# A constant-matmul warm-up and a new order table for windowed attention with a gated convolution

## The chip, the cores and the metric

The kernel runs on one core of a Trainium2 chip. Its metric is device time in microseconds: the median of several executions. One more execution is profiled. The profile's times count from its first instruction, and its span, 239.8 us here, is a little shorter than the time of that execution, 241.62 us.

## The reference

Four batches, eight heads, 768 positions, head width 64. Every query sees its neighbours at a distance under 16 and, for each of 24 blocks of 32 keys, one summary: the maximum of the block's keys, and the mean of its values. The heads side by side are the input `x` (512 wide) of the second half: a causal convolution of five taps in each channel gives a gate, and the gated value product goes through an output product.

```python
k_sum = k.reshape(B, H, nb, 32, D).max(axis=3)
v_sum = v.reshape(B, H, nb, 32, D).mean(axis=3)
s_l = where(abs(i - j) < 16, scale * q @ k.T, -1e9)
s_s = scale * q @ k_sum.T + log(32)
a = softmax(concatenate([s_l, s_s], -1))
attn = a @ concatenate([v, v_sum], 2)
x = attn.transpose(0, 2, 1, 3).reshape(B, S, H * D)
gate = sigmoid(sum(conv_w[t] * xp[:, t:t + S] for t in range(5)))
out = (gate * (x @ w_val)) @ w_out
```

## The kernel before

The work is cut into 12 groups `g` (four batches, three stretches of 256 positions), and each group into two units `u` of four heads. Every unit and group passes through the same steps, and each step has a letter. The letters with their numbers stand in one long table, `ORDER`, and the program is emitted in that order: each engine executes its own instructions in the order of the table, so the table is the schedule. There is no other planner at run time; semaphores make an instruction wait for its inputs and for its buffer.

The steps of a unit are: `S` scores on TensorE (two halves), `N` mask and row minimum on VectorE (four steps, each of two masked scores), `E` exponentials with row sums on ScalarE (four steps of two), `R` sum and reciprocal on VectorE, `M` normalisation on POOL, `T` transposes on TensorE, `C` their copies on ScalarE, `X` the product with the values on TensorE, then on ScalarE `F` and `H` (two copies of the result) and `I` (the last convolution tap), and `A` on VectorE (the four further taps of each of two halves, eight steps). `G` is the gate on ScalarE. The steps of a group are: `V` the value product (two halves), `gf` gate times value on VectorE, `gh` and `gl` its split into two parts on ScalarE and POOL, `O` the output product (two halves), `oe` its eviction and `st` its store. Group 0 uses plain float32 products. For it the convolution of the first unit is a matmul, `Z`.

Beside these run the preparations: `k`, `q0`, `q`, `v`, `n`, `w`, `o`, `c`, `m`, `i` are loads on SyncE's queue; `ks` is the block maximum of a piece of keys on VectorE and `kc` copies it beside the keys on POOL; `VB` sums the first batch's values with a matmul against a constant of ones, `vb` copies the sums; `tr` sums the values of later batches on POOL or VectorE; `wvs`, `wvd`, `wve` (and `wos`, `wod`, `woe`) turn one quarter of the float64 value (output) weights into float32: a ScalarE step, then a VectorE step that takes the low bits (line 356), then a VectorE step that joins both (line 366). `O.0.1` and `O.0.0` need all four joins of the output weights.

A piece of keys is 478 KB, a quarter of the first queries 128 KB, the mask 180 KB, the convolution weights 20 KB. The first product of scores, `S.0.0`, needs `k.0.0`, its maximum copied beside it, and `q0.0`.

## Time and profile before

| | us |
|---|---|
| median of three runs | 242.12 |
| lowest and highest | 240.76, 245.85 |
| the profiled execution | 241.62 |
| its span | 239.8 |
| TensorE busy | 224.0 |
| ScalarE busy | 186.4 |
| VectorE busy | 171.5 |
| POOL busy | 152.6 |

Busy time is the time in which an engine has an instruction in work; for TensorE, whose matmuls are pipelined, a group's time is best read from its start to the start of the next. A float32 matmul appears as two records. Below, "PE" is TensorE, "PEld" its weight loads, "DVE" VectorE, "ACT" ScalarE, "SP" SyncE.

### The profile page before, as it was taken

Reading aid. Unit: us, or ns where it says so; the run is one execution under the profiler, and the core shown is the slowest. Engines: PE = TensorE matmul, PEld = TensorE weight load, DVE = VectorE, ACT = ScalarE, POOL = GpSimd, SP = SyncE. Lnnn points to the kernel's source line nnn. Section 1 sums busy time; section 2 is a strip of 40 time slices with the busy share of each in tenths; the row PEclk is TensorE's granted clock in tenths of the full one; section 3 lists DMA queues with packets and bytes.
Section 4 is the critical chain, followed back from the end, with each engine's and each line's share of the span. In section 5 each row is a group of like instructions: output and inputs, shape, how many; then the busy total and the mean of one; then the engine's idle time right before and its main releaser. Section 6 shows DMA issues by size and latency. Waiting matters only on the chain.

```text
span 239.8 us, 7765 instructions
## 1 busy us (share of the span) xinstructions
PE 224.0 (93%) x2880; PEld 187.0 (78%) x2880; DVE 171.5 (71%) x676; ACT 186.4 (78%) x612; POOL 152.6 (64%) x216
## 2 busy tenths in 40 slices
PE   0596999899999999999999999999999999999993
PEld 0233988778489889889879898879889889978982
DVE  1568699899999998788877878848396655264300
ACT  0199989999999999899989999889898863443321
POOL 1219699887998996896986974936238728017400
PEclk9999999999999999999999999999999999999999
DMA  6999998989699847364834836235044131102022
GB/s 176 376 396 405 404 383 257 407 278 389 192 324 326 303 154 208 73 243 115 297 125 122 304 101 197 105 77 178 8 120 174 24 100 44 44 3 105 26 92 87
DMA packets 17318, 46.42 MB, mean 194 GB/s; under 512 B 2400, under 2 KB 3424, under 8 KB 17280
## 3 DMA queue, kind: packets, MB, share of 16 engines
q1 hardware_dynamic: 17280, 45.93, 55.8%
q8 instruction: 23, 0.38, 0.6%
q14 instruction: 15, 0.12, 0.2%
HBM read 37.46 MB, written 6.29 MB: 182 GB/s over the span
## 4 chain that ended last, share of the span: by engine, by line
PE 73%; DMA 11%; DVE 7%; SPq 3%; ACT 2%; issue 1%; POOL 1%; DVEq 0%; ACTq 0%
PE out L580 30%; PE val L551 25%; PE x L471 8%; PE s L401 6%; PE pt L454 4%; DMA k<-in_kT_dram 4%; DMA qbd<-in_qT_dram 3%; DMA vn<-in_vn_dram 3%; DMA v<-in_vw_dram 2%; DVE g L505 2%; DVE sn L417 2%; SPq L325 1%; ACT p L432 1%; DVE wf L366 1%; DVE low_wo L356 1%
## 5 line engine op out<-in xcount | busy, mean ns | idle before, releaser
L505 DVE SCALAR_TENSOR_TENSOR g<-xf,cwt,g 128x256 f32<-128x256 f32 x184 | 89.4, 486 | 27.7 <-ACT g L500 23.3
L432 ACT ACTIVATE p<-sn,nm 128x120 f32<-128x120 f32 x192 | 74.0, 394 | 0.8 <-DVE nm L417 0.8
L445 POOL TENSOR_TENSOR p<-p,nm 128x480 f32<-128x480 f32 x48 | 46.9, 988 | 19.6 <-DVE nm L440 13.4
L551 PE MATMUL val<-xh,wv 128*128 128x256 f32 x352 | 50.0, 284 | 0.0
L417 DVE CUSTOM_DVE_ANT_0 sn<-s,mask 128x120 f32<-128x120 f32 x192 | 43.0, 276 | 5.9 <-PE s L401 4.8
L551 PEld LDWEIGHTS val<-xh,wv 128*128 128x128 f32 x352 | 45.1, 188 | 1.6 <-issue 0.4
L580 PE MATMUL out<-wo,gh 128*128 128x512 f32 x176 | 45.9, 402 | 0.0
L565 POOL TENSOR_TENSOR gl<-gf,gh 128x512 fp32r<-128x512 f32 x22 | 28.4, 1291 | 18.9 <-ACT gh L560 18.9
L491 POOL TENSOR_TENSOR xl<-xf,xh 128x512 fp32r<-128x512 f32 x22 | 28.4, 1290 | 17.9 <-ACT xh L483 15.9
L432 ACT ACTIVATION_READ_ACCUMULATOR p<-sn,nm 128x1 f32 x192 | 38.1, 198 | 0.0
L580 PEld LDWEIGHTS out<-wo,gh 128*128 128x128 f32 x176 | 31.7, 188 | 7.4 <-issue 0.3
L401 PE MATMUL s<-k,qbd 64*64 64x120 f32 x768 | 27.2, 278 | 8.4 <-POOL k L271 8.4
L401 PEld LDWEIGHTS s<-k,qbd 64*64 64x64 f32 x768 | 20.7, 138 | 16.4 <-POOL k L271 8.4
L471 PE MATMUL x<-pts,v 120*64 120x64 f32 x768 | 29.4, 225 | 2.9 <-ACT pts L458 2.9
L471 PEld LDWEIGHTS x<-pts,v 120*64 120x64 f32 x768 | 26.1, 137 | 6.8 <-ACT p L432 2.0
L458 ACT COPY pts<-pt 120x512 f32<-120x512 f32 x48 | 27.7, 588 | 3.7 <-PE x L471 2.3
L282 POOL TENSOR_TENSOR vT<-vT 128x384 f32<-128x384 f32 (+3 forms) x44 | 24.9, 566 | 6.5 <-DMA vT<-in_vT_dram 3.8
L551 PE MATMUL val<-xl,wv 128*128 128x256 f32 x176 | 27.9, 281 | 0.0
L556 DVE SCALAR_TENSOR_TENSOR gf<-gt,val 128x512 f32<-128x512 f32 x24 | 16.3, 683 | 10.8 <-PE val L551 7.4
L551 PEld LDWEIGHTS val<-xl,wv 128*128 128x128 f32 x176 | 23.9, 188 | 0.0
L580 PE MATMUL out<-wo,gl 128*128 128x512 f32 x88 | 23.9, 393 | 0.0
L590 ACT ACTIVATE ob<-out 128x512 f32<-128x512 f32 x23 | 13.9, 604 | 10.9 <-PE out L580 10.6
(58 smaller groups left out, 267.2 us busy)
## 6 DMA issues: line engine op xcount, KB each, us to landing
v<-in_vw_dram SPq DMA_DIRECT2D x24, 512.0 KB
k<-in_kT_dram SPq DMA_DIRECT2D x16, 478.0 KB
out_dram<-ob SPq DMA_DIRECT2D x23, 256.0 KB
qbd<-in_qT_dram SPq DMA_DIRECT2D x11, 512.0 KB
vT<-in_vT_dram SPq DMA_DIRECT2D x12, 384.0 KB
raw_wv<-in_wv_dram SPq DMA_DIRECT2D x4, 512.0 KB
raw_wo<-in_wo_dram SPq DMA_DIRECT2D x4, 512.0 KB
v<-vs SPq DMA_DIRECT2D x36, 48.0 KB
```

The costliest lines, as they stand in the source:

```text
L282: nc.gpsimd.tensor_tensor(dst, src[:, :, :n], src[:, :, n : 2 * n], ALU.add)
L401: nc.tensor.matmul(sp[64 * e : 64 * e + 64, h, c * KW : c * KW + KW], qbd[g % NQB][64 * h : 64 * h + 64, pr, i * QT : i * QT + QT], ktile( ...
L417: nc.vector.tensor_tensor_reduce(sn[:, n, :], tiles["s", u][:, h, c * KW : c * KW + KW], mask[:, mv, :], -1.0 / math.sqrt(D), 3.0e38, ALU.add,
L432: nc.scalar.activation(p[:, n, :], tiles["sn", u][:, n, :], AF.Exp, bias=tiles["nm", u][:, n : n + 1], scale=-1.0, accum_out=rs[:, n, :1],)
L445: nc.gpsimd.tensor_tensor(p[:, w], p[:, w], ri[:, w].unsqueeze(2).broadcast_to([P, TPU, KW]), ALU.mult)
L458: nc.scalar.copy(pts[:, :, QT * e : QT * e + QT], tiles["pt", u][:KW, e])
L471: nc.tensor.matmul(dst, v[:KW, i, c0 : c0 + D], src, start=True, stop=g > 0)
L491: nc.gpsimd.tensor_tensor(xl[:, prs(u), :], xf(g)[:, prs(u), HALO:], tiles["xh", g][:, prs(u), :].bitcast(F32), ALU.subtract,)
L505: nc.vector.scalar_tensor_tensor(gt, xf(u // NHP)[:, pr, o : o + SG], cwt[:, pr, o : o + 1], gt, ALU.mult, ALU.add)
L551: nc.tensor.matmul(ps[:, r], w, x, start=(n == 0), stop=(n == len(terms) - 1))
L565: nc.gpsimd.tensor_tensor(gl[:, cos, :], tiles["gf", g, cp], tiles["gh", g][:, cos, :].bitcast(F32), ALU.subtract)
L580: nc.tensor.matmul(ps, x, w, start=(n == 0), stop=(n == len(terms) - 1))
```

## The change

A new step `D` is added: two float32 matmuls of 104 by 104 on the tile of ones, into the buffer that the transposes use later; nobody reads the result. It is called twelve times, ahead of all other matmuls. The order table is another one altogether; the list of steps in it is otherwise the same, except that one sum of values (`tr.1.3`) goes to VectorE instead of POOL, `tr.2.3` goes to VectorE, and the ScalarE or POOL side of some weight splits is swapped.

```diff
 ORDER = """
-k.0.1 mset c k.0.0 q0.0 k.0.2 q0.1 m n.0.2 cd ks.0.1 q0.2 k.0.3 ks.0.0 n.0.3 q0.3 kc.0.0 kc.0.1
-S.0.0 ks.0.2 n.0.4 w.3 S.0.1 n.0.1 kc.0.2 q.1 VB.2 N.0.2 n.0.5 E.0.2 N.0.1 N.0.0 E.0.0 i N.0.3
...
+k.0.0 mset q0.0 m k.0.1 D.8 i D.11 k.0.2 q0.1 D.10 q0.2 ks.0.0 c D.2 kc.0.0 D.5 n.0.2 D.3 k.0.3
+D.4 D.0 D.9 D.6 D.1 D.7 ks.0.1 q0.3 S.0.0 w.0 N.0.1 kc.0.1 E.0.1 ks.0.2 n.0.0 S.0.1 q.1 n.0.5
...
+    def op_D(i):
+        t = once("warm", lambda: ps_t.tile([P, 2, NP, QT], F32, tag="pt", name="warm"))
+        n = QT + BASE
+        for k in range(2):
+            nc.tensor.matmul(
+                t[:n, k].rearrange("p a b -> p (a b)")[:, :n],
+                tiles["ones"][:, :n], tiles["ones"][:, :n], start=True, stop=True,
+            )
+
...
-        c=op_c, ks=op_ks, kc=op_kc, tr=op_tr, VB=op_VB, vb=op_vb, VS=op_VS,
+        c=op_c, ks=op_ks, kc=op_kc, tr=op_tr, VB=op_VB, D=op_D, vb=op_vb, VS=op_VS,
```

TensorE at the start of the program, first before and then after (`s` are scores, `vb` the sums of the first batch's values, `warm` the new step; in a name the first number is the unit, in `k` the batch and the piece):

```order
L401 MATMUL s_0_122<-k_0_0_99,qbd0_81 64x120 x8
L401 MATMUL s_0_122<-k_0_1_88,qbd0_81 64x120 x8
L296 MATMUL vb_0_150<-vn_1_106,ones_90 64x512
L296 MATMUL vb_1_152<-vn_1_106,ones_90 64x512
L401 MATMUL s_1_173<-k_0_2_102,qbd0_81 64x120 x8
```

```order
L309 MATMUL warm_101<-ones_90 104x104 x24
L410 MATMUL s_0_144<-k_0_0_88,qbd0_81 64x120 x8
L410 MATMUL s_0_144<-k_0_1_99,qbd0_81 64x120 x8
L296 MATMUL vb_0_184<-vn_1_123,ones_90 64x512
L296 MATMUL vb_1_186<-vn_1_123,ones_90 64x512
L410 MATMUL s_1_198<-k_0_2_107,qbd0_81 64x120 x8
L410 MATMUL s_1_198<-k_0_3_127,qbd0_81 64x120 x8
```

The 24 constants stand ahead of the first scores, and both halves of unit 1's scores now follow the first sums together.

TensorE around the first output product `O.0.1` (`out_0_1`), before and after (`val` is `V`, `pt` is `T`, `x` is `X`; lines are nine higher in the new file):

```order
L551 MATMUL val_1_1_951<-xh_1_715,wv_344 128x256 x8
L551 MATMUL val_1_1_951<-xl_1_790,wv_344 128x256 x4
L551 MATMUL val_1_1_951<-xh_1_715,wv_344 128x256 x8
L551 MATMUL val_1_1_951<-xl_1_790,wv_344 128x256 x4
L401 MATMUL s_9_1000<-k_1_2_283,qbd0_81 64x120 x8
L401 MATMUL s_9_1000<-k_1_3_447,qbd0_81 64x120 x8
L454 MATMUL pt_6_1022<-ident_84,p_6_777 120x64 x16
L471 MATMUL x_5_1043<-pts_5_908,v_2_618 64x64 x16
L580 MATMUL out_0_1_1074<-wf_87,gf_0_0_665 128x512 x2
L580 MATMUL out_0_1_1074<-wf_87,gf_0_1_857 128x512 x2
```

```order
L463 MATMUL pt_5_881<-ident_84,p_5_602 120x64 x16
L410 MATMUL s_8_910<-k_1_0_313,qbd0_81 64x120 x8
L410 MATMUL s_8_910<-k_1_1_422,qbd0_81 64x120 x8
L480 MATMUL x_4_937<-pts_4_867,v_2_672 64x64 x16
L589 MATMUL out_0_1_987<-wf_87,gf_0_0_722 128x512 x2
L589 MATMUL out_0_1_987<-wf_87,gf_0_1_821 128x512 x2
L589 MATMUL out_0_0_1003<-wf_87,gf_0_0_722 128x512 x2
L589 MATMUL out_0_0_1003<-wf_87,gf_0_1_821 128x512 x2
L463 MATMUL pt_6_1035<-ident_84,p_6_774 120x64 x16
L480 MATMUL x_5_1058<-pts_5_1013,v_2_672 64x64 x16
L410 MATMUL s_9_1083<-k_1_2_465,qbd0_81 64x120 x8
L410 MATMUL s_9_1083<-k_1_3_530,qbd0_81 64x120 x8
```

Unit 9's scores, unit 6's transposes, unit 5's product and a half of group 1's value product stood ahead of the output product and now stand behind it.

VectorE at the last joins of the output weights (`wf`), before and after (`low_wo` holds the low bits, `g` is a tap):

```order
L356 TENSOR_SCALAR low_wo_2_996<-raw_wo2_846 128x512
L505 SCALAR_TENSOR_TENSOR g_3_976<-xf_1_620,cwt_85,g_3_976 128x256
L366 SCALAR_TENSOR_TENSOR wf_87<-sc_wo2_998,low_wo_2_996 128x512
L356 TENSOR_SCALAR low_wo_1_1041<-raw_wo1_842 128x512
L505 SCALAR_TENSOR_TENSOR g_3_976<-xf_1_620,cwt_85,g_3_976 128x256
L366 SCALAR_TENSOR_TENSOR wf_87<-sc_wo1_992,low_wo_1_1041 128x512
```

```order
L514 SCALAR_TENSOR_TENSOR g_2_748<-xf_1_646,cwt_85,g_2_748 128x256
L365 TENSOR_SCALAR low_wo_3_980<-raw_wo3_871 128x512
L375 SCALAR_TENSOR_TENSOR wf_87<-sc_wo3_967,low_wo_3_980 128x512
L426 ISA sn_8_969,nm_8_970<-s_8_910,mask_83 128x120
```

The last join stood among the taps of unit 3 and now follows the last tap of unit 2.

## Rows read from the trace of the kernel before

**Rows 1.** The page: busy time of each engine with its share of the span, and the granted TensorE clock in 40 slices (9 is 90% of full or more).

```profile
PE 224.0 (93%) x2880; PEld 187.0 (78%) x2880; DVE 171.5 (71%) x676; ACT 186.4 (78%) x612; POOL 152.6 (64%) x216
...
PEclk9999999999999999999999999999999999999999
```

**Rows 2.** The chain of work that ended last, in order of time: start in us, duration in us, engine, tile and line.

```profile
58.77 0.60 DVE wf L366
...
59.51 3.67 PE out L580 x8
63.18 0.98 PE s L401 x32
...
67.79 2.84 PE val L551 x24
70.63 0.61 PE pt L454 x16
...
72.22 1.08 PE x L471 x32
...
225.03 11.16 PE out L580 x48
...
236.26 0.60 ACT ob L590
```

**Rows 3.** TensorE's timeline at the start: start in us, busy us, and in brackets the idle time before and what ended it.

```profile
8.42 2.09 PE L401 MATMUL s<-k,qbd 64*64 64x120 f32 x32 [8.42 <-POOL k L271]
...
13.50 1.74 PE L296 MATMUL vb<-vn,ones 128*64 128x512 f32 x4
15.17 0.64 PE L401 MATMUL s<-k,qbd 64*64 64x120 f32 x16
...
18.59 1.94 PE L296 MATMUL vb<-vn,ones 128*64 128x512 f32 x8
...
23.96 0.34 PE L471 MATMUL x<-pts,v 120*64 120x64 f32 x4 [1.84 <-ACT pts L458]
```

**Rows 4.** Busy time of each engine in three stretches (stretch, its length, PE, PEld, DVE, ACT, POOL, then granted clock, DMA share, GB/s), and VectorE's waits in the first 60 us (us in total, times, longest).

```profile
0.00:59.37 59.37, 47.44 (x792) 35.40 (x792) 45.98 (x209) 46.66 (x171) 38.16 (x71) 1.00 0.95 346
59.51:236.19 176.68, 176.58 (x2088) 151.61 (x2088) 125.34 (x468) 139.02 (x441) 114.29 (x146) 1.00 0.45 145
...
8.42:59.51 51.09, 47.45 (x793) 35.44 (x793) 44.13 (x206) 46.80 (x171) 36.91 (x59) 1.00 0.98 367
...
DVE ks L258 <- DMA k<-in_kT_dram: 4.7, 4, 2.0
DVE cwt L356 <- DMA cwraw<-in_cw_dram: 4.6, 1, 4.6
DVE sn L417 <- PE s L401: 3.1, 5, 1.3
```

**Rows 5.** The timeline of VectorE (first row) and ScalarE (the others): the first masked score, the table load behind it, the first two exponentials, and the first and the last of ScalarE's four small waits up to 35 us.

```profile
10.57 0.28 DVE L417 CUSTOM_DVE_ANT_0 sn<-s,mask 128x120 f32<-128x120 f32 x1 [0.52 <-PE s L401]
...
10.95 1.28 ACT L432 ACT_TABLE_LOAD   x1 [10.95 <-DVE nm L417]
12.24 0.39 ACT L432 ACTIVATE p<-sn,nm 128x120 f32<-128x120 f32 x1
...
12.63 0.38 ACT L432 ACTIVATE p<-sn,nm 128x120 f32<-128x120 f32 x1
...
16.61 0.39 ACT L432 ACTIVATE p<-sn,nm 128x120 f32<-128x120 f32 x1 [0.27 <-DVE nm L417]
...
34.85 0.59 ACT L486 COPY xf<-x 128x512 f32<-128x512 f32 x1 [0.72 <-PE x L473]
```

**Rows 6.** What VectorE's steps take in the chain (a tap before a tap, a masked score, a tap before a masked score, a reciprocal, a block maximum), and from the groups by line the sum of values (count, busy us, mean ns).

```profile
45.44 0.49 DVE g L505
45.93 0.18 DVE sn L417
...
46.32 0.41 DVE g L505
...
52.59 0.20 DVE nm L440
...
53.56 0.86 DVE ks L258
...
L278 DVE TENSOR_REDUCE vsT<-vT 128x24 f32<-128x768 f32 x1 | 0.9, 902 | 0.0
```

**Rows 7.** The start on POOL (the constants) and VectorE (the second and the third block maximum).

```profile
0.98 0.48 POOL L209 MEMSET ones<- 32x1 f32 x4
...
6.91 0.95 DVE L258 TENSOR_REDUCE ks<-k 128x24 f32<-128x768 f32 x1 [1.31 <-DMA k<-in_kT_dram]
...
9.10 0.95 DVE L258 TENSOR_REDUCE ks<-k 128x24 f32<-128x768 f32 x1 [1.24 <-DMA k<-in_kT_dram]
```

**Rows 8.** TensorE's timeline at the float32 product of line 530 and the group behind it, and the weight loads of that product (count, busy us, mean ns).

```profile
27.59 4.58 PE L530 MATMUL g<-xf,dg 128*128 128x256 f32 x20
32.10 0.64 PE L401 MATMUL s<-k,qbd 64*64 64x120 f32 x16
...
L530 PEld LDWEIGHTS g<-xf,dg 128*128 128x128 f32 x20 | 3.7, 189 | 0.6 <-issue 0.2
```

**Rows 9.** The timeline at the end: VectorE's half of the one tile that is evicted in halves.

```profile
233.89 0.42 DVE L588 TENSOR_SCALAR ob<-out 128x256 f32<-128x256 f32 x1 [8.03 <-ACT ob L587]
```

More of the change, by code (lines that the diff above doesn't have):

```diff
@@ new lines @@
+M.0.1 S.2.1 n.1.0 E.1.2 VB.5 N.2.1 n.1.3 M.0.0 E.2.1 N.2.2 VB.1 N.2.3 E.2.3 N.2.0 w.1 wve.0 S.3.0
+E.2.0 k.1.0 R.1 S.3.1 E.2.2 w.3 T.0 M.1.1 N.3.0 VB.4 C.0.0 R.2 N.3.1 v.1.0 C.0.1 M.2.0 VB.3 N.3.3
+wvs.2 N.3.2 wvd.2 M.2.1 v.1.1 S.4.0 vb.1 S.4.1 wve.2 vb.0 M.1.0 T.2 E.3.3 N.4.1 k.1.1 X.0 N.4.0
+wvc.2.1 E.3.2 N.4.2 k.1.2 C.2.0 cs C.2.1 ce N.4.3 W.0 T.1 F.0 tr.1.0.1 E.4.1 S.5.0 S.5.1 tr.1.3
+W.1 n.1.1 wvs.1 Z.0.0 k.1.3 E.3.0 wvd.1 wvc.0.1 E.3.1 wve.1 C.1.0 R.3 Z.0.1 wvs.3 wvd.3 M.3.1
+C.1.1 wve.3 E.4.0 wvb.2 N.5.0 N.5.3 wvc.1 ks.1.0 f.1.1.1 X.1 E.5.0 wvc.3.1 n.1.2 N.5.2 E.5.3
@@ new lines @@
+wos.0 k.2.0 wod.0 k.2.3 S.8.0 H.3 v.3.1 wod.1 S.8.1 E.6.3 L.3 v.3.0 X.4 woe.0 n.2.2 E.7.3 woe.1
+H.4 A.2.6 q.5 woc.1.1 wos.3 N.8.1 A.2.7 tr.2.0 wod.3 G.2 F.4 woe.3 O.0.1 I.3.0 N.8.2 E.7.0 A.3.0
+R.6 E.7.2 O.0.0 A.3.1 M.6.1 ks.2.1 I.3.1 C.5.0 h.2 A.3.2 M.6.0 E.7.1 N.8.0 A.3.3 C.5.1 kc.2.1
+N.8.3 oe.0.1 L.2 A.3.4 woc.3 R.7 T.6 A.3.5 E.8.3 f.3.0.0 M.7.0 X.5 A.3.6 E.8.1 A.3.7 v.4.0 ks.2.3
+S.9.0 G.3 f.3.1.1 S.9.1 I.4.1 ks.2.0 kc.2.3 V.1.0 f.3.1.0 I.4.0 M.7.1 E.8.0 A.4.0 f.3.0.1 A.4.1
+L.4 woc.0 N.9.3 q.6 oe.0.0 A.4.2 k.2.2 C.6.0 st.0.1 A.4.3 E.8.2 V.1.1 N.9.0 A.4.4 H.5 N.9.2 F.5
@@ new lines @@
+st.1.0 O.2.1 F.9 A.8.7 n.3.1 ks.3.0 G.8 L.9 I.9.1 gf.3.0 I.9.0 h.5 N.14.1 E.13.0 M.11.1 A.9.0
+N.14.0 VS.2 E.13.2 L.8 A.9.1 T.11 ks.3.1 oe.2.1 X.10 E.14.2 M.12.1 A.9.2 C.11.0 A.9.3 S.15.0
+M.12.0 E.13.3 A.9.4 S.15.1 V.4.1 gh.3.0 N.15.1 C.11.1 A.9.5 gl.3.0 vs.2 N.15.2 A.9.6 gh.3.1
+f.6.0.0 R.13 kc.3.0 F.10 A.9.7 gl.3.1 q.9 G.9 V.4.0 f.6.0.1 I.10.0 gf.4.1 M.13.1 f.6.1.1 E.14.0
+N.15.0 A.10.0 st.2.1 h.6 M.13.0 N.15.3 I.10.1 f.6.1.0 E.14.1 A.10.1 tr.3.1 T.12 A.10.2 H.10 S.16.0
+A.10.3 E.15.3 S.16.1 A.10.4 E.14.3 X.11 A.10.5 A.10.6 E.15.0 v.7.1 tr.3.2 N.16.1 O.3.0 n.3.3 F.11
@@ new lines @@
+A.15.1 E.18.3 N.19.1 A.15.2 E.19.0 h.8 A.15.3 M.17.1 E.19.3 oe.4.0 S.20.0 gf.6.1 S.20.1 A.15.4
+gh.6.1 T.17 N.20.3 E.19.1 VS.3 A.15.5 V.7.1 N.20.1 vs.3 N.20.2 C.17.0 A.15.6 f.9.1.0 N.20.0 A.15.7
+f.9.0.1 R.18 G.15 st.3.1 E.19.2 S.21.0 f.9.1.1 S.21.1 gh.6.0 f.9.0.0 X.16 C.17.1 gl.6.0 N.21.3
+E.21.3 st.4.0 N.21.0 N.21.1 O.5.1 I.16.0 M.18.0 N.21.2 F.16 E.21.2 A.16.0 gl.6.1 gf.7.1 I.16.1
+H.16 A.16.1 M.18.1 E.21.0 A.16.2 S.22.0 S.22.1 A.16.3 E.21.1 T.18 A.16.4 E.20.3 A.16.5 X.17 N.22.2
+N.22.0 v.10.0 V.7.0 A.16.6 H.17 v.10.1 N.22.1 F.17 A.16.7 C.18.0 R.19 G.16 R.21 M.19.1 oe.5.1
@@ new lines @@
+I.17.0 O.5.0 E.20.0 M.19.0 A.17.0 N.22.3 I.17.1 L.17 C.18.1 A.17.1 E.20.2 A.17.2 L.16 A.17.3
+f.10.1.1 A.17.4 T.19 f.10.0.0 A.17.5 E.22.1 M.21.0 S.23.0 gf.7.0 S.23.1 E.20.1 A.17.6 X.18 E.22.0
+N.23.2 A.17.7 V.8.1 oe.5.0 N.23.0 gh.7.0 N.23.1 st.5.0 R.20 gh.7.1 st.5.1 gl.7.0 f.10.0.1 E.22.2
+f.10.1.0 G.17 M.20.0 O.6.1 H.18 gf.8.1 E.22.3 h.9 gl.7.1 C.19.0 R.22 I.18.1 M.20.1 I.18.0 F.18
+O.7.1 M.21.1 oe.6.1 A.18.0 C.19.1 A.18.1 A.18.2 A.18.3 A.18.4 T.20 A.18.5 E.23.1 X.19 A.18.6
+A.18.7 oe.7.1 N.23.3 V.8.0 C.20.0 st.7.1 G.18 v.11.0 C.20.1 v.11.1 I.19.0 H.19 E.23.0 O.7.0 F.19
@@ L128 @@
+H.22 O.8.0 gf.10.0 A.22.2 A.22.3 V.10.1 gh.10.0 gh.9.1 gl.10.0 I.22.1 oe.8.0 A.22.4 gl.9.1 st.8.0
+A.22.5 X.23 gf.10.1 L.22 A.22.6 O.9.0 F.23 A.22.7 gh.10.1 H.23 gl.10.1 G.22 L.23 O.10.1 oe.9.0
+I.23.0 st.9.0 I.23.1 st.8.1 A.23.0 A.23.1 A.23.2 V.11.0 A.23.3 A.23.4 oe.10.1 A.23.5 A.23.6
+st.10.1 A.23.7 O.9.1 G.23 gf.11.0 V.11.1 oe.9.1 gh.11.0 st.9.1 O.10.0 gf.11.1 gh.11.1 gl.11.1
+gl.11.0 O.11.0 oe.10.0 st.10.0 O.11.1 oe.11.0 st.11.0 oe.11.1 st.11.1
 """
```

111 lines of the change are left out of this document (38 added, 73 removed).

## The prediction

> **What bounds the kernel now.** I read the chain of waits first, in order of time. From 59.51 us to 236.19 us it is TensorE and nothing else: one group of matmuls behind the other, ending with the output product of the last stretch [rows 2]. TensorE is also the busiest engine of the page, at 224.0 us [rows 1]. So the end of the kernel is one sum: the moment at which the first output product (`O.0.1`, line 580) starts, plus the TensorE work that stands behind it in the program, 176.7 us in the kernel before, plus the last eviction and store. What set that moment is the row ahead of it in the chain: VectorE's last join of the output weights (line 366), which started at 58.77 us [rows 2]. Nothing of TensorE itself was late.
>
> The second view is TensorE's own timeline at the start [rows 3]. Its first 32 score records take 2.09 us, and the same 32 take 0.98 us later in the chain [rows 2]; four sum records (line 296) take 1.74 us at 13.50 us, where later eight take 1.94 us. The granted-clock line reads full throughout [rows 1], but by these durations the array ran at 1.2 GHz from 8.42 us to about 14.9 us (by its length some 1.4 us of that group is still slow) and at 2.4 GHz from there on. The work of 8.42 to 15.17 us, 48 score and eight sum records, takes 1.5 + 1.9 us at the later pace, so the slow stretch costs 3.3 us of TensorE time. TensorE was never idle in it.
>
> Then I asked what VectorE and ScalarE were short of before 59.4 us. VectorE worked 45.98 us of the first 59.37 us [rows 4], so it lost 13.4 us: 4.6 us for the first load, 4.7 us for four loads of `k`, 3.1 us for score tiles. ScalarE's first exponential starts at 12.24 us, behind a table load of 1.28 us, and it hardly waits after that: four small waits, 0.2 to 0.7 us each, 1.4 us in all by 35 us [rows 5].
>
> **The change, part by part.** (1) It adds 24 matmuls of 104 columns to TensorE, before the first scores, on constants that POOL has written by 1.46 us [rows 7]. No row shows this shape. The nearest is the full-width float32 product of line 530: ten matmuls (20 records) of 256 columns from 27.59 us to the next group at 32.10 us [rows 8], 0.45 us each, so 0.183 us for 104 columns at 2.4 GHz and 0.37 us at 1.2 GHz. From above: if the weight load (189 ns a record there, two records to a matmul) were not hidden, some 0.35 us more each. I take the lower price, since in line 530 the load is hidden. If the clock needs as long as before, 6.5 us from the first matmul, it rises at 8.1 us: 17.7 matmuls by then, the other 6.3 in 1.15 us. The constants end at 9.2 us; between 7.9 us (the clock rises at 5 us) and 10.4 us (it never does).
>
> (2) It moves the loads: `k.0.0` is first, with queries and mask ahead of the second `k`. In the kernel before VectorE could take the second `k` at 6.91 us, with 976 KB in the queue up to it, and the third at 9.10 us, with 1582 KB [rows 7]. The second is now at 1264 KB, so 7.95 us, and its reduction ends at 8.9 us. The first score tile follows the constants: 9.2 to 9.7 us. The first masked score starts at 9.76 us, the table load 0.38 us behind it (10.57 to 10.95 us before [rows 5]), and the first exponential at **11.4 us instead of 12.24**. It cannot be ahead of 10.6 us (the reduction at 8.9 us) and is at 12.6 us if the clock stays low.
>
> (3) VectorE's start follows ScalarE's. Ahead of the first tap `A.1.0` VectorE has 24.5 us of work in the new order (24 masked pairs 9.6 us, seven reductions of `k` 6.1 us, eight weight steps 5.2 us, two sums of `v` 1.8 us, small ones 1.8 us), and what `A.1.0` waits for, `I.1.0` on ScalarE, has 24.4 us ahead of it (40 exponentials at 0.38 us and 9.2 us of copies). So VectorE loses at least what ScalarE loses: 11.4 us and some 0.2 us of small waits, **11.6 us instead of 13.4**. Ends: 10.6 and 12.8 us.
>
> (4) The order around `O.0.1` is the core. VectorE has less ahead of the last join: four taps (0.45 us each, between the 0.41 us in front of a masked score and 0.49 us in front of a tap), three masked pairs of 0.40 us, one reduction of `k` at 0.87 us, one 0.26 us sum and reciprocal; and one sum of `v` more, 0.90 us [rows 6]. That is 3.2 us less (3.1 to 3.4 us with the cheapest and the dearest taps), so 42.8 us. TensorE loses more cover: scores 9 (0.98 us), transposes 6 (0.61 us), product 5 (1.08 us) and half a value product (2.84 us) [rows 2] now stand behind `O.0.1`, **5.5 us**. So the join comes earlier, and more is left to do behind it.
>
> (5) The tail: the last output tile is now the one that is evicted in two halves beside each other, the longer one 0.42 us [rows 9], instead of 0.60 us [rows 2]. That gives 0.2 us. All other moves I cost at nothing: behind `O.0.1` TensorE is the bound, with 139.0 us of ScalarE and 125.3 us of VectorE work under 176.7 us [rows 4], and by the same counts of work the new order has every producer there at least 2.5 us ahead. SyncE's queue has the last quarter of the output weights as its 48th transfer, as before; its last quarter landed in time for VectorE then, and I cost it at nothing; were it late, VectorE and `O.0.1` would wait as long as it is.
>
> **The sum.** `O.0.1` starts at 42.8 + 11.6 + 0.14 = 54.5 us (59.51 before; 0.14 us from the join's end to the first matmul). Behind it 176.7 + 5.5 = 182.2 us: 236.7 us. The tail is 3.6 - 0.2 = 3.4 us: span 240.1 us, and with the 1.8 us that the profiled execution has around its span (241.62 against 239.8) **241.9 us**. The profiled execution lies 0.5 us under the median of the three runs, 242.12, so the forecast is 0.3 us over the one and 0.2 us under the other: no change. With the ends above it goes from 240.7 to 243.2 us.
>
> **A rule of the Trainium skill.** The row gives 3.3 us for the slow stretch, 1.4% of the span [rows 3]. The Trainium skill (TensorE: Matmul & The Clock Gate, Part 1) says that the array starts throttled until activity releases it, and that for modelling this costs under 1% of a typical kernel. By the row a full return would be 3.3 us, by the page under 2.4 us; the sum above uses neither, because in it the time goes to waiting for VectorE.
>
> **Rivals.** First, *TensorE decides, and the slow stretch comes back.* For it: in the 51.1 us from 8.42 us TensorE idled only 3.6 us [rows 4], so the front is nearly its own. Then 241.6 - 3.3 - 0.2 = 238.1 us, and up to 3.6 us less if the new order also closes its idle time: 234.5 us. Against it: the chain names VectorE ahead of 59.51 us, and 5.5 us of TensorE work was put behind that point.
>
> Second, slower: *TensorE cools in the gap that the new order opens.* The last work ahead of `O.0.1` is `S.8` and `X.4`; `S.8` waits for the masked scores of unit 7, with 37.8 us of VectorE work up to them, so it starts at 37.8 + 11.6 = 49.4 us, and 0.98 + 1.08 us later TensorE has nothing left: from 51.5 us it waits 3.0 us for the join; its longest gap after the start was 1.84 us, at 23.96 us, and the clock held [rows 3]. If the clock falls there, `O.0.1` and `O.0.0` (7.3 us) and the next products run at 1.2 GHz; at the start the same cost 3.3 us: 245.2 us. It decides only if the gap is longer than any in this trace. The Trainium skill (the same page, Why this matters for your kernels) warns of idle gaps between bursts of matmuls; no row here shows a fall.
>
> Third, *the constants do not raise the clock.* They end at 10.4 us, ScalarE starts at 12.6 us, and the sum is 243.1 us; the slow scores are then hidden in the 8 us that TensorE idles before `O.0.1` anyway.
>
> **How the numbers follow.** Forecast 0.55, first rival 0.29, second 0.11, third 0.05. A measurement of this kernel tells about 2% from no change: 237.3 and 247.0 us. Half of the first rival lies under 237.3 us, which gives 0.15 for faster; half of the second, with a second gap like it, over 247.0 us, 0.06 for slower; 0.79 for the same. The range takes in the near end of the first rival and most of the second, and the unknown waits of VectorE (one like its longest for `k`, 2.0 us, would give 243.9 us [rows 4]): 238.0 to 245.0 us.
>
> **What would show it.** Score records of line 410 at about 0.5 us for 16 from the first one on; the constants ending near 9.2 us; the first exponential near 11.4 us; `O.0.1` near 54.5 us with an idle gap of some 3 us in front of it and an unbroken TensorE behind. The prediction is wrong if that gap is missing (VectorE's work is cheaper than priced, or the other rows in front of the join moved), or if TensorE waits a second time after it.

## The result, and the profile after

The changed kernel takes **243.84 us** (median of 18 executions, 241.78 to 246.3); the kernel before, measured beside it, 241.67 us (18 executions). The ratio is **1.0073**, 95% interval 1.0047 to 1.0099: no change at 2%, but slower, where the forecast said no change with a time 0.2 us under the 242.12 us of the three runs. The time lies in the forecast's range. (Ratios here leave out executions over 1.5% above the fastest of their kernel, so they can differ from the quotient of the medians.)

The profiled execution took 242.41 us (span 240.6), 1.4 us *less* than the median; that of before, 241.62 us, was at its median. The page and the chain of the changed kernel, the latter in order of time (start, us, what), answer to [rows 1] and [rows 2]:

```profile
PE 228.6 (95%) x2928; PEld 193.5 (80%) x2928; DVE 172.2 (72%) x678; ACT 186.6 (78%) x612; POOL 147.5 (61%) x206
...
q8 instruction: 23, 0.38, 0.6%
```

```profile
1.50 7.47 PE warm L309 x48
8.98 0.61 PE s L410 x16
...
9.99 1.28 ACT L441
11.29 5.40 ACT p L441 x28
...
53.43 0.68 DVE wf L375
54.16 7.14 PE out L589 x16
...
99.25 5.69 DMA out_dram<-ob
...
228.77 8.30 PE out L589 x36
237.14 0.39 ACT ob L596
```

The start is as reckoned: constants to 8.97 us, scores at the fast pace from the first on (0.61 us for 16 in the chain; 0.64 us in the timeline, as at 15.17 us in [rows 3]), first exponential at 11.29 us, first output product at 54.16 us. But the chain behind it is no longer TensorE alone: at 99.25 us it runs over a store. And the idle gap of 3 us ahead of 54.16 us is missing. TensorE's timeline (start, busy, in brackets the idle time before and what ended it) shows where TensorE idled instead, to be held against [rows 3]:

```profile
12.43 0.64 PE L410 MATMUL s<-k,qbd 64*64 64x120 f32 x16 [0.56 <-issue]
14.13 0.64 PE L410 MATMUL s<-k,qbd 64*64 64x120 f32 x16 [1.06 <-POOL xf L395]
...
23.29 1.21 PE L410 MATMUL s<-k,qbd 64*64 64x120 f32 x32 [0.97 <-DVE low_wv L365]
...
27.11 0.68 PE L463 MATMUL pt<-ident,p 64*120 64x64 f32 x16
29.81 1.05 PE L410 MATMUL s<-k,qbd 64*64 64x120 f32 x32 [2.02 <-DVE low_wv L365]
30.79 4.59 PE L539 MATMUL g<-xf,dg 128*128 128x256 f32 x20
...
105.67 1.22 PE L560 MATMUL val<-xh,wv 128*128 128x256 f32 x8 [0.37 <-ACT ob L599]
...
109.12 1.22 PE L560 MATMUL val<-xh,wv 128*128 128x256 f32 x8 [0.35 <-ACT vs L325]
...
113.99 1.15 PE L480 MATMUL x<-pts,v 120*64 120x64 f32 x32 [0.17 <-ACT xh L492]
```

Two places ask for a reason. The first is **28 us**: 2.02 us of idle time ahead of `S.5`. The view names VectorE's `low_wv`, but `S.5` does not read it. It needs the score buffer, that is, the last masked score of unit 4, and VectorE's timeline has that done at 26.5 us, before `low_wv` starts. The first weight load of `S.5` (the line PEld), the first of its instructions, also ran ahead of the stop:

```profile
26.19 0.28 DVE L426 CUSTOM_DVE_ANT_0 sn<-s,mask 128x120 f32<-128x120 f32 x1
26.39 1.81 DVE L278 TENSOR_REDUCE vsT<-vT 128x24 f32<-128x768 f32 x2
28.11 0.68 DVE L365 TENSOR_SCALAR low_wv<-raw_wv 128x512 uint32<-128x512 uint32 x1
...
27.72 0.13 PEld L410 LDWEIGHTS s<-k,qbd 64*64 64x64 f32 x1
```

The second is **102 to 114 us**. ScalarE's eviction of `O.2.1` waited 2.30 us for a buffer whose store had not landed, and TensorE lost 0.9 us in three pieces behind it:

```profile
105.02 0.60 ACT L599 ACTIVATE ob<-out 128x512 f32<-128x512 f32 x1 [2.30 <-DMA out_dram<-ob]
```

The busy times by stretch (length; PE, PEld, DVE, ACT, POOL; granted clock) answer to [rows 4]: 182.9 us from the first output product to the last matmul, 182.0 of them busy.

```profile
54.16:237.07 182.91, 182.01 (x2192) 156.74 (x2192) 131.54 (x495) 145.74 (x460) 116.26 (x146) 1.00 0.48 152
8.91:54.16 45.25, 39.15 (x690) 29.43 (x689) 38.34 (x181) 40.45 (x152) 29.80 (x48) 1.00 0.98 360
```

That accounts for the profiled execution, 0.8 us over before: 54.16 + 182.0 + 0.9 + 3.5. It does not account for the medians, 2.2 us apart. Each execution comes with its mean granted clock, and there is a hint in them: of the changed kernel's 18 executions nine have a clock of 0.997 or more (median 243.17 us) and nine less, down to 0.976 (median 244.94). Of 29 executions of the kernel before, in the first group of experiments, 24 have 0.997 or more (241.28 us) and five 0.992 or 0.993 (242.88 us). The clock alone is not the difference, since the executions at 0.997 or more are still 1.9 us apart.

### The profile page after: what moved, and what is told of

Same layout as the page of the kernel before. It is cut to its first block, busy times and chain, and to the rows that moved or that the text cites. A ratio compares the mean times of both kernels' runs of the same rounds, so it can differ in the third digit from the quotient of the medians.

```text
span 240.6 us, 7861 instructions
## 1 busy us (share of the span) xinstructions
PE 228.6 (95%) x2928; PEld 193.5 (80%) x2928; DVE 172.2 (72%) x678; ACT 186.6 (78%) x612; POOL 147.5 (61%) x206
## 4 chain that ended last, share of the span: by engine, by line
PE 72%; ACT 12%; DVE 8%; issue 3%; DMA 2%; POOL 2%; ACTq 0%; POOLq 0%; DVEq 0%
PE out L589 26%; PE val L560 25%; PE x L480 8%; ACT p L441 7%; PE s L410 5%; PE pt L463 4%; PE warm L309 3%; DMA out_dram<-ob 2%; DVE sn L426 2%; DVE g L514 2%; ACT pts L467 1%; DVE wf L375 1%; DVE ks L258 1%; POOL vT L282 1%; ACT xh L492 1%
## 5 line engine op out<-in xcount | busy, mean ns | idle before, releaser
L514 DVE SCALAR_TENSOR_TENSOR g<-xf,cwt,g 128x256 f32<-128x256 f32 x184 | 89.3, 485 | 26.5 <-ACT g L509 15.5
L574 POOL TENSOR_TENSOR gl<-gf,gh 128x512 fp32r<-128x512 f32 x22 | 28.3, 1292 | 36.1 <-ACT gh L569 27.8
L426 DVE CUSTOM_DVE_ANT_0 sn<-s,mask 128x120 f32<-128x120 f32 x192 | 43.7, 276 | 8.5 <-ACT p L441 3.6
L589 PE MATMUL out<-wo,gh 128*128 128x512 f32 x176 | 44.7, 396 | 0.0
L500 POOL TENSOR_TENSOR xl<-xf,xh 128x512 fp32r<-128x512 f32 x22 | 28.3, 1290 | 15.0 <-ACT xf L495 11.2
L410 PE MATMUL s<-k,qbd 64*64 64x120 f32 x768 | 25.8, 269 | 5.4 <-DVE low_wv L365 3.0
L410 PEld LDWEIGHTS s<-k,qbd 64*64 64x64 f32 x768 | 20.2, 133 | 11.4 <-issue 4.4
L282 POOL TENSOR_TENSOR vT<-vT 128x384 f32<-128x384 f32 (+3 forms) x36 | 20.4, 565 | 2.1
```

The source lines that it names most:

```text
L282: nc.gpsimd.tensor_tensor(dst, src[:, :, :n], src[:, :, n : 2 * n], ALU.add)
L410: nc.tensor.matmul(sp[64 * e : 64 * e + 64, h, c * KW : c * KW + KW], qbd[g % NQB][64 * h : 64 * h + 64, pr, i * QT : i * QT + QT], ktile( ...
L426: nc.vector.tensor_tensor_reduce(sn[:, n, :], tiles["s", u][:, h, c * KW : c * KW + KW], mask[:, mv, :], -1.0 / math.sqrt(D), 3.0e38, ALU.add,
L500: nc.gpsimd.tensor_tensor(xl[:, prs(u), :], xf(g)[:, prs(u), HALO:], tiles["xh", g][:, prs(u), :].bitcast(F32), ALU.subtract,)
L514: nc.vector.scalar_tensor_tensor(gt, xf(u // NHP)[:, pr, o : o + SG], cwt[:, pr, o : o + 1], gt, ALU.mult, ALU.add)
L574: nc.gpsimd.tensor_tensor(gl[:, cos, :], tiles["gf", g, cp], tiles["gh", g][:, cos, :].bitcast(F32), ALU.subtract)
```

## The experiments

Medians are of up to 12 timed executions; "before" is the kernel before on the same chip, in the same group of runs.

### First group: constants, store, front and back apart

**No constants in the changed kernel.** Edit: the twelve `D` out of the table.

> The changed kernel without its 24 constant matmuls, the order otherwise as changed. The first half of the scores can then start at about 5.5 us, when POOL's copy of the first maxima ends, instead of 8.91 us. Theory A (the constants bring 3.3 us of fast clock, and the new order gave them back as TensorE's waits for VectorE at 10 to 54 us): scores and sums run slow again to about 15 us, but VectorE and ScalarE, which set the start of the first output product, start no later, so that product starts within 0.7 us of 54.16 us and the span is 239.9 to 241.3 us. Theory B (TensorE decides, the constants' 3.3 us are in the result): the first output product starts 2 to 3 us later and the span is 242.6 to 243.9 us. Theory C (the medians lie 1.4 us further apart than the profiled executions because a TensorE that starts at full pace is granted less clock later in some executions): here the granted clocks of the timed executions are 0.998 to 1.000 and the median lies within 0.5 us of the profiled execution.

Measured: 242.64 us, before 241.50; ratio 1.0054 (1.0026 to 1.0082). First output product at 54.46 us, convolution group at 27.99 us: no stop at 28 us. It stopped instead for 1.80 us ahead of `S.8` at 50.99 us (for a load, see the fourth group), and the granted clock was 0.54 over the 3.4 us behind that stop. Theory A and B asked for a span under 241.3 or over 242.6 us; it was 242.1, with that fall in it, and nine of twelve executions at full clock had a median of 242.45 us. So the constants do not bring 3.3 us; C is half right: nine clocks were 0.997 or more, three 0.992 or 0.993.

**Constants in the kernel before.** Edit:

```diff
+D.0 D.1 D.2 D.3 D.4 D.5 D.6 D.7 D.8 D.9 D.10 D.11
 S.0.0 ks.0.2 n.0.4 w.3 S.0.1 n.0.1 kc.0.2 q.1 VB.2 N.0.2 n.0.5 E.0.2 N.0.1 N.0.0 E.0.0 i N.0.3
```

> The kernel before with the 24 constant matmuls ahead of its first scores and nothing else changed. The constants end near 9.0 us, so the first scores start 0.5 us later than before (8.42 us) and take 1.0 us instead of 2.09 us. Theory A: VectorE's first masked score starts 0.3 to 0.5 us earlier (10.57 us before) and loses a little less behind the scores; the first output product, which waits for VectorE's joins, comes 0.3 to 1.0 us earlier than 59.51 us; span 238.8 to 239.5 us. Theory B: it comes 2.8 us earlier, span 237.0 us. Theory C: granted clocks under 0.99 in some of the timed executions, and a median over 1 us above the profiled execution.

Measured: 242.25 us, before 241.50; ratio 1.0026 (0.9988 to 1.0063). Theory B falls: nothing gained. One of the twelve executions took 366.36 us at a mean granted clock of 0.562; the kernel before has one like it in the last group of runs (316.92 us at 0.667), so it need not come from the edit. In the profiled execution the first exponential came 0.65 us earlier (11.59), but TensorE's timeline shows a stop in the middle of a group of scores, with nothing to wait for between its 9th and 10th matmul record:

```profile
43.72 0.52 PE L410 MATMUL s<-k,qbd 64*64 64x120 f32 x9
45.89 1.48 PE L410 MATMUL s<-k,qbd 64*64 64x120 f32 x23 [1.66 <-issue]
```

The granted clock was 0.50 from 46 to 49 us, and the first output product started at 62.21 us, 2.7 us later and not 0.3 to 1.0 us earlier as theory A had it.

**The store of O.1.1 earlier.** Edit: `st.1.1` ahead of `f.5.1.1` on SyncE's queue.

> The changed kernel with one store (st.1.1, the second half of group 1's output) issued ahead of the first copies of the value sums of group 5 instead of some 70 steps later, so that the eviction of O.2.1 has a free buffer. In the changed kernel ScalarE waits 2.3 us for a store at 102.7 to 105.0 us and TensorE then idles 0.37, 0.35 and 0.17 us. Theory A: that wait goes, TensorE is unbroken behind the first output product, span 239.7 us (0.9 us less). Rival: the copies of the sums stand behind the store on SyncE's queue and TensorE waits for them instead; span 240.4 us or more. Theory D (the store's landing time, which differs from execution to execution, is why the median lies 1.4 us above the profiled execution): the median falls by 2 us or more, to 241.8 us or less; without D it falls by 0.9 us.

Measured: 242.78 us, before 241.50; ratio 1.0022 (0.9986 to 1.0058). ScalarE's wait for the store is gone, but now TensorE waited for another transfer at the same place (the rival), and the median is 1.1 us lower, not the 2 us of theory D. Nine of the twelve executions had a clock under 0.997; in the profiled one the stop at 28 us was there again, with a fall of the clock behind it (windows: length, busy times, clock last but two):

```profile
29.28 1.37 PE L410 MATMUL s<-k,qbd 64*64 64x120 f32 x32 [1.74 <-DVE low_wv L365]
...
105.36 1.15 PE L480 MATMUL x<-pts,v 120*64 120x64 f32 x32 [1.01 <-issue]
```

```profile
29.00:32.00 3.00, 2.72 (x35) 2.16 (x35) 2.04 (x5) 3.00 (x12) 1.01 (x2) 0.65 1.03 412
```

**The new front with the old back.** Edit: the changed table up to `oe.0.1`, then the remaining steps in the order of before.

> The changed order up to the eviction of O.0.1 (the first output product and its partner included), and from there the steps that remain in the order of the kernel before. Theory A (the new front moves the first output product 5.35 us forward and puts 5.5 us of TensorE work behind it: nothing gained; the slip of 0.9 us lies in the new back): first output product at 54.2 us as in the changed kernel, TensorE unbroken behind it, no tail in halves: span 239.9 us. If the slip lies in the new front: span 240.6 us or more with an unbroken back. If the old back does not fit the new front (it was written for another state of the buffers): idle time of TensorE in 55 to 100 us, span above 241 us.

Measured: 251.68 us (six executions), before 241.50; ratio 1.0387 (1.0329 to 1.0445). The third case: the old back does not fit, TensorE idled 3.54 and 2.33 us at 69 to 77 us and the clock fell. The front could not be judged by it, only that its stop at 28 us was there again (2.01 us).

### Second group: the gaps filled

I took the clock's falls to come from idle gaps, and filled these.

```diff
+    def op_U(i):            # two more constant matmuls, into the convolution's buffer
...
+U.0 U.1 U.2
 S.1.1
...
+U.3 U.4 U.5 U.6
 S.4.0
...
+U.7 U.8 U.9 U.10 U.11 U.12 U.13
 S.5.0
```

> The changed kernel with more constant matmuls in three of TensorE's idle gaps: three steps of two ahead of S.1.1 (1.06 us idle at 14.13 us in the changed kernel's profile), four ahead of S.4.0 (0.97 us at 23.29 us) and seven ahead of S.5.0 (2.02 us at 29.81 us). They write a buffer that is free until the first convolution; nobody reads it. By the step D at the fast clock (0.067 us a record, four records a step) the 14 steps take 3.7 us, inside 4.05 us of idle time. Theory E (in half of the executions the clock falls to 1.2 GHz behind such a gap: 9 of 18 executions of the changed kernel had a mean granted clock under 0.997, and in the profile of the kernel with the early store the clock was 0.65 from 29 to 32 us behind an idle gap of 1.74 us): every execution has a granted clock of 0.997 or more, and the median falls from 243.8 to 242.4 to 243.2 us. Rival F (the clock falls for another reason, say because TensorE works more): still about half of the executions under 0.997, median 243.8 us or, with the fillers' 3.7 us on top, more.

> The changed kernel with the fillers of the run before and with the early store as well. Theory: both add up. Clock 0.997 or more in every execution, no wait of ScalarE for a store near 103 us, TensorE unbroken behind the first output product: 0.9 us under the kernel with the fillers alone, median 241.5 to 242.3 us, which is no more than the kernel before (241.5). If only the store's wait moves elsewhere: the same median as with the fillers alone.

> The kernel before with seven filler steps ahead of X.0, where its TensorE idles 1.84 us at 23.96 us, and nothing else changed. 24 of its 29 executions had a granted clock of 0.997 or more (median 241.28 us), the other five 0.992 or 0.993 (median 242.88 us). Theory E: those five vanish if they come from this gap; median 241.3 us, highest under 243.2 us. If they come from its second gap (1.05 us at 43.37 us) or from elsewhere, one execution in six stays near 242.9 us.

Measured: fillers in the changed kernel 245.61 us (six executions; ratio 1.0154, 1.0100 to 1.0209), with the early store 243.78 us (1.0090, 1.0055 to 1.0124), in the kernel before, ahead of `X.0`, 242.55 us (1.0045, 1.0020 to 1.0071); before 241.38. On the clock theory E held in the main: five of six, nine of eleven and twelve of twelve executions had 0.997 or more. On the time it failed. The fillers seem to cost more than the gaps they sat in: I had priced a record at 0.067 us, but the constants of the change take 0.09 at the fast clock, so 14 steps take 5.0 us, not 3.7, in 4.05 us of gaps; the first output product came at 55.40, 54.96 and 60.11 us instead of 54.16 and 59.51. And the executions of the first at full clock still lay between 243.2 and 246.8 us, so there something besides the clock and the fillers varied; with the early store the profiled execution had TensorE unbroken behind the first output product (242.1 us, the fastest of eleven), and what the slower ones waited for no trace of mine shows.

**The first half of the scores earlier**, on top of the fillers and the early store. Edit: `S.0.0`, `N.0.0`, `N.0.1` and their exponentials ahead of `ks.0.1`, six of the constants behind `S.0.0`; `S.1.0`, `N.1.0`, `N.1.1` ahead of `ks.0.3`.

> The kernel of the run before with the start reordered: six of the twelve constant steps ahead of S.0.0 and six behind it, so that the first half of the scores runs at about 5.6 us instead of 8.91, and its four masked scores and their exponentials stand ahead of the second block maximum (VectorE idles 2.80 us there in the changed kernel); the first half of unit 1's scores and masks stands ahead of the fourth block maximum. Theory G (behind 10 us TensorE waits for VectorE and ScalarE, so what they start earlier is gained): first exponential at 8.3 to 8.6 us instead of 11.29; VectorE has 0.8 us less to do behind the second block maximum, ScalarE 1.6 us; TensorE's idle time from 9 to 54 us falls by 0.8 to 1.6 us, the median is 240.3 to 241.5 us. Rival (the loads of k set the pace of the first 14 us whatever stands ahead of them): the first output product as in the run before and the same median, 241.5 to 242.3 us.

Measured: 243.61 us (six executions), before 241.38; ratio 1.0119 (1.0069 to 1.0170). The first exponential came at 8.24 us, 3 us earlier, and nothing was gained: the third block maximum started at 9.22 us and the fourth at 13.15 us, the first output product at 55.82 us. The rival held in the time (243.78 us in the run before). But the pace was not set by the loads of `k` alone: the third maximum waited 0.56 us for POOL, and ahead of the scores whose masks stand before the fourth TensorE waited 1.02 us for a load of queries and 0.38 us for one of values. Its profile shows the wait behind 100 us at its worst, and the clock behind it:

```profile
106.97 1.57 PE L489 MATMUL x<-pts,v 120*64 120x64 f32 x32 [1.90 <-issue]
```

```profile
107.00:111.00 4.00, 4.00 (x67) 3.58 (x68) 0.48 (x5) 2.73 (x7) 3.00 (x5) 0.57 0.46 159
```

### Third group: the instruction stream and SyncE's queue

Where a stop has no wait, what else could hold TensorE? The page lists a queue that carries instructions, 23 packets of 0.38 MB in all. One begins just ahead of 27.2 us (a window from 27.1 to 27.2 us; its share of 16 engines' time, 66.8% of 0.1 us, makes 1.07 us of one engine). It begins ahead of the stop, which runs from 27.8 to 29.8 us, and ends inside it, at 28.3 us:

```profile
q8 instruction: 1, 0.02, 66.8%
```

The stop also stood behind the same record in every kernel with that front: 344 matmuls and 345 weight loads, the last column pairs of this stretch up to the stop.

```profile
0.00:27.75 27.75, 22.90 (x344) 16.78 (x345) 17.19 (x98) 16.76 (x68) 10.66 (x28) 1.00 0.95 350
```

The transfers: behind `f.5.1.1`, the first copy of group 5's value sums, the new table sends `q.8`, `n.3.2` and `v.6.1` (512, 384 and 512 KB) between the four small copies that `X.10` waits for, and the store behind `v.6.0`.

```diff
-    for k in range(2): matmul(t[:n, k] ... [:, :n], ones[:, :n], ones[:, :n])
+    matmul(t[:n, i % 2] ... [:, : 4 * n], ones[:, :n], ones[:, : 4 * n])     # 8 steps, not 12
```

```diff
-f.5.1.1 ... q.8 ... f.5.1.0 ... n.3.2 ... f.5.0.1 ... v.6.1 ... f.5.0.0 ... v.6.0
+st.1.1 f.5.1.1 f.5.1.0 f.5.0.1 f.5.0.0 ... q.8 ... n.3.2 ... v.6.1 ... v.6.0
```

> The changed kernel with its constants as 8 matmuls of 416 columns instead of 24 of 104: about the same time of TensorE (by the sums of the first values, 0.49 us a record at the slow and 0.27 us at the fast clock for 512 columns, some 6 us), but 64 records fewer in TensorE's instruction stream. Theory H: in the changed kernel TensorE stops at 27.8 us for 2.0 us although the only thing that S.5 waits for, the last masked score of unit 4, was done at 26.4 us; the kernels with the early store and with the new front alone, which have the same stream up to there, stop at the same record (the 689th, counting weight loads) for 1.7 and 2.0 us, and the kernel without constants and the ones with fillers do not stop there. A packet of the queue that carries instructions lies in each such stop (27.1 to 28.2 us here), so TensorE waits for its own instructions, which come late among the loads. Then the stop vanishes here, since that place of the stream now lies in the slow matmuls of the convolution: convolution group at 28.3 to 29.2 us instead of 30.79, fewer executions with a granted clock under 0.997 (at most 3 of 12, against 9 of 18), first output product at 52.5 to 53.9 us, median 241.8 to 243.0 us. Rival V (it is VectorE, as the table of waits names it: the low bits of a value weight): VectorE's work is the same, the stop of 2 us stays at S.5 and half of the executions stay under 0.997; median 243.8 us.

> The same, and on SyncE's queue the store of O.1.1 and all four copies of group 5's value sums stand ahead of the loads q.8, n.3.2, v.6.1 and v.6.0 (1.9 MB) that stood between and ahead of them. Theory J: at 103 to 108 us every kernel with the new back waits for these transfers by an amount that changes from execution to execution (TensorE idle 0.9 us in the changed kernel, 1.0 with the early store, 1.7 without constants, 1.9 with the early first half), which is why executions at full clock spread over 2.6 us and more. Then no idle time of TensorE over 0.3 us behind the first output product, a spread of the executions at full clock under 1.5 us, and a median 0.9 to 1.5 us under the kernel with the wide constants alone: 240.6 to 241.8 us. Rival: the loads that are now later are waited for instead; same median as with the wide constants alone.

> The changed kernel with the new order of the transfers alone, constants as in the change. Theories H and J: the stop at S.5 stays (1.7 to 2.0 us, half of the executions under 0.997), the one at 103 to 108 us goes; the median is 0.9 to 1.5 us under the changed kernel, 242.3 to 242.9 us. If the spread at full clock comes from the front alone, the median stays at 243.8 us.

Measured, before 241.37 us: wide constants 244.03 us (six executions; ratio 1.0106, 1.0061 to 1.0152); wide constants and the new order of transfers 241.19 us (0.9998, 0.9972 to 1.0024); the new order of transfers alone **242.02 us** (1.0010, 0.9979 to 1.0040).

Theory J held in the main. With the transfers reordered TensorE has no idle time of 0.2 us or more behind the first output product in either kernel; of the new order alone:

```profile
53.84:235.51 181.67, 181.66 (x2192) 156.64 (x2192) 131.65 (x495) 145.74 (x460) 116.31 (x146) 1.00 0.47 151
```

The eight executions at full clock (0.997 or more) of the kernel with both changes lie within 240.81 and 241.42 us, and its median is 2.8 us under that of the wide constants alone, more than the 0.9 to 1.5 forecast. Alone the new order takes the ratio from 1.0073 to 1.0010, and the median at full clock from 243.17 to 240.93 us. One point failed: its seven executions at full clock still spread from 239.75 to 243.81 us, so these transfers are not all of the spread. Since the early store alone had left 1.01 us ahead of `X.10`, and the sums' copies together with the store left none, both were in it.

Theory H missed its forecast for the wide constants: the convolution group started at 30.93 us and not by 29.2, the median is 244.03 us and not 241.8 to 243.0, and three of six executions have a clock under 0.997. The thing itself it had right: the stop did not vanish with 64 records fewer, it **moved by 64 records**, from ahead of `S.5` (64 records long) to behind it, ahead of the convolution:

```profile
27.88 1.05 PE L409 MATMUL s<-k,qbd 64*64 64x120 f32 x32
30.93 4.59 PE L538 MATMUL g<-xf,dg 128*128 128x256 f32 x20 [1.99 <-issue]
```

```profile
0.00:28.90 28.90, 24.32 (x344) 13.69 (x344) 17.63 (x99) 17.62 (x72) 11.44 (x28) 1.00 0.96 353
```

Rival V, which had the stop stay at `S.5`, falls.

**Wide constants in the kernel before.** Edit: eight such steps ahead of `S.0.0`.

> The kernel before with 8 wide constants ahead of its first scores. With 24 narrow ones its TensorE stopped for 1.66 us in the middle of a group of scores (behind record 1195, at 44.2 us, with a packet of instructions from 43.2 to 44.4 us), and the clock then fell for 3.4 us in the profiled execution. Theory H: the stop moves to another place or goes; where it goes the span is under the kernel before by what the constants bring, 0.3 to 1.5 us: median 240.0 to 241.2 us. Rival: the constants bring nothing to a front that VectorE sets; median 241.4 us, and with a stop elsewhere 242 us or more.

Measured: 241.36 us, before 241.37; ratio 0.9999 (0.9971 to 1.0027). No stop without a named wait is left in the front; the first output product came 0.64 us earlier (58.87), and the last matmul ended at 236.20 us as before (236.17): the stretch behind the product was 177.3 us instead of 176.7. The rival held: the constants bring nothing to the time.

### Fourth group: the stop moved on purpose

> The kernel with the new order of the transfers (store and sums of group 5 ahead of the loads), with 9 of the 12 constant steps: 24 records fewer in TensorE's stream. In the changed kernel and in five others the stop of 1.7 to 2.1 us near 28 us stands behind record 688 or 689; with 64 records fewer it moved from ahead of S.5 to ahead of the convolution group. Theory H (the place in the stream decides): now it falls into the middle of S.5, behind its 12th of 32 matmul records, where no instruction waits for another engine; some 2 us, beginning 0.4 us later than ahead of S.5. Rival V (a wait for VectorE or a load): the stop stays ahead of S.5's first matmul or goes. Median as with the back alone, 241.0 to 242.5 us.

Edit: three of the twelve `D` out (24 records), with the reordered transfers. Measured: 243.05 us, before 241.41; ratio 1.0068 (1.0041 to 1.0095), a little over what I expected, since in seven of its twelve executions the clock was under 0.997. The stop came where the count put it, behind the 12th matmul record of a group in which nothing waits for another engine, and the clock fell to half behind it:

```profile
27.25 0.63 PE L410 MATMUL s<-k,qbd 64*64 64x120 f32 x12
30.08 0.83 PE L410 MATMUL s<-k,qbd 64*64 64x120 f32 x20 [2.21 <-issue]
30.85 4.33 PE L539 MATMUL g<-xf,dg 128*128 128x256 f32 x11
```

```profile
31.00:34.00 3.00, 3.00 (x8) 2.37 (x9) 2.90 (x16) 3.00 (x14) 2.82 (x5) 0.50 1.04 407
```

That settles it: the place in TensorE's own stream decides, not VectorE.

The traces show more of it when the other records of TensorE's own stream (semaphore waits, and a drain at the start) are counted with its matmuls and weight loads. In all seven kernels that stop near 28 us, 705 records stand ahead of the stop, and in the kernel before with narrow constants 1217 stand ahead of its stop at 44.2 us: 512 more, two packets' worth by an estimate from the page (23 packets for some 5,900 records of TensorE, about 256 each). In each of these eight TensorE went on 1.3 to 1.5 us behind the end of the packet: the second packet at 705, the fourth at 1217. In no trace here does the record behind the 705th, or behind any 256th from there on, start sooner than 1.27 us behind the end of its packet.

> No constants, and the new order of the transfers: 96 records fewer, so the stop near 28 us lies in the convolution's slow matmuls and does not show, as in the first experiment (convolution group at 28.0 us instead of 30.8). That experiment had a second stop of 1.8 us ahead of S.8 (behind record 1248, a packet of instructions from 47.8 to 48.9 us), a slow stretch behind it and 2.06 us of waits at 104 to 116 us. Theory H and J: the waits at 104 to 116 us go, the stop ahead of S.8 stays and the clock falls behind it in some executions: span 239.0 to 240.0 us, median 240.6 to 241.8 us, which is within 0.5 us of the kernel before (241.4). If the stop at S.8 was a load, it may go too: median 239.5 us.

> As the run before, with two wide constants (416 columns, 16 records with their weight loads), so 80 records fewer than the changed kernel. They end near 4 us, too early to raise the clock for the scores. Theory H: near 28 us the stop lies 16 records into the convolution (8 of its matmul records, 1.8 us), so at most 0.3 us of it shows; the second stop, behind record 1248, now lies 16 records earlier in the program, inside the transposes ahead of S.8. Span and median as in the run before within 0.7 us. If both stops vanish or shrink: median 239.5 to 240.5 us, under both kernels.

Edits: no `D`, or two wide ones, and the reordered transfers. Measured: **240.62 us** without constants (ratio **0.9967**, 0.9946 to 0.9988) and **240.32 us** with two (0.9967, 0.9942 to 0.9993). Both are under both kernels. The stop at 28 us does not show, since its place lies in the slow matmuls of the convolution (group at 28.41 us without constants; 30.14 us with two wide ones, with no idle time ahead of it). Without constants 0.72 and 1.13 us of idle time ahead of `T.5` and `S.8` remained, with two wide ones 0.30 and 0.16 us. The stop ahead of `S.8` is another thing. In the runs without constants it stands behind 1272 records, which is no such place, and the view names VectorE, which is again not what it waited for. `S.8` needs the load `q.4`, the queries of group 4, which stands in SyncE's queue behind the output weights `o.0`. Its last part landed at 51.25 us, and `S.8` started at 51.39 us (50.85 and 50.99 us without constants in the first group); with two wide constants the view names the load. What `T.5` waited for stays open. The lines are of `S.8` without constants and with two wide ones:

```profile
51.39 1.05 PE L410 MATMUL s<-k,qbd 64*64 64x120 f32 x32 [1.13 <-DVE low_wo L365]
...
51.32 1.05 PE L409 MATMUL s<-k,qbd 64*64 64x120 f32 x32 [0.16 <-DMA qbd<-in_qT_dram]
```

The stretch behind the first output product is unbroken (no constants):

```profile
53.45:235.03 181.58, 181.58 (x2196) 156.69 (x2192) 130.95 (x490) 145.90 (x460) 115.70 (x145) 1.00 0.47 155
```

The run with two wide constants is also the plainest word on the slow start: its TensorE ran at half clock for most of 10 to 20 us, and its median is the lowest of all, though not to be told from the run without constants.

```profile
10.00:15.00 5.00, 3.93 (x44) 1.67 (x40) 3.79 (x24) 4.45 (x24) 0.94 (x5) 0.50 1.02 381
15.00:20.00 5.00, 5.00 (x52) 2.39 (x49) 1.83 (x18) 2.93 (x13) 1.93 (x2) 0.57 1.05 407
```

## Why the prediction was wrong

Step by step, against the profiled execution of the changed kernel:

- *Constants end at 9.2 us*: 8.97. Right by its terms: counted from the start (length, busy, records, clock), some 5.8 records a microsecond at first, 0.35 us a matmul (0.37 reckoned), 11 from about 7.5 us on (8.1 reckoned), 0.18 us a matmul (0.183). The clock column reads 1.00 in both. In the profiles of the other kernels with twelve steps they ended at 7.6 to 9.0 us; by the prediction's own prices its lower end, 7.9 us, should have been 7.6.

```profile
0.00:6.50 6.50, 5.00 (x29) 1.00 0.68 188
0.00:7.50 7.50, 6.00 (x34) 1.00 0.73 217
0.00:8.50 8.50, 7.00 (x45) 1.00 0.76 236
```

- *First exponential 11.4 us*: 11.29. Right. *O.0.1 at 54.5 us*: 54.16. Near, but partly by luck: VectorE worked 40.2 us up to there, not 42.8, and lost 13.9 us, not 11.6, and the two errors nearly cancel. Two loads of `k` alone cost it 6.8 us.
- *An idle gap of 3 us ahead of O.0.1*: missing, 0.25 us. `S.8` started at 51.77 us, not 49.4. TensorE had spent that time before, in the stop of 2.02 us at 28 us and in 0.97 us at 23 us, and from 29.81 us to the product it was busy for 23.61 of 24.35 us.
- *182.2 us unbroken behind it*: 182.0 us of work, right, but 0.9 us of idle time in it. **This is the first step that failed**: "All other moves I cost at nothing", because every producer's engine was 2.5 us ahead. I counted the engines' work and not SyncE's queue, although the table moves its transfers too: three of the group's four sums went behind up to 1.4 MB of loads, and a store behind them. Undoing that is worth 1.0073 against 1.0010 in ratio, some 1.5 us; the same step takes 1.0106 to 0.9998 with wide constants and 1.0054 to 0.9967 without constants. That is more than the 0.9 us of the profile; the wait differs from profile to profile (0 to 2.3 us in those without this repair), which may be why.
- *The last quarter of the output weights in time*: right, VectorE waited for no load of them. (By the trace it is the 51st transfer that SyncE issues, the 52nd before, and not the 48th.)
- *Tail 3.4 us*: 3.5. Right.
- *Span plus 1.8 us is the time*: true of the profiled execution (242.41 against 241.9 forecast), not of the median, 1.4 us above it. **The second step that failed** is the price of the 24 matmuls: I costed their time, which lies in idle time, and not that they are 96 records more in TensorE's instruction stream. With them the place at which the stream runs dry came into a fast stretch ahead of `S.5`; TensorE stops there for 2 us in the profiles, and half of the executions have a clock under 0.997. With the transfers repaired, taking the constants out too brings the ratio from 1.0010 (0.9979 to 1.0040) to 0.9967 (0.9946 to 0.9988), another 1.0 us. This step is smaller and less sure than the first: the intervals overlap a little, and without the repair 1.0073 and 1.0054 cannot be told apart. Most of it seems to be the clock and not the 2 us themselves: the first output product starts at 53.84 us with the stop and at 53.45 without, the medians at full clock are 240.93 and 240.42 us, and five of twelve executions against one of twelve are under 0.997.

The rivals. The first, that the slow stretch of 3.3 us comes back, is refuted twice: constants in the kernel before bring nothing (0.9999), and the kernels with the lowest medians have a slow start. So the argument of the sum, that this time goes into waiting, was right. The second, that TensorE cools in a gap, named the right mechanism at the wrong place: behind stops of 1.7 to 2.2 us the clock fell to 1.2 GHz for about 3 us, in some profiles and not in others (in the changed kernel's own it held). The third, that the constants do not raise the clock, is out: their pace doubled at about 7.5 us.
